# A convolution and a two-layer dense net on one core: dense part in two eras of seven weight blocks, array fills in unbroken chains

## The chip, the cores and the metric

One core of one Trainium2 chip runs the kernel. The metric is the device time of one execution in microseconds (us). TensorE is called PE here, VectorE DVE, ScalarE ACT, GpSimd POOL and SyncE SP, as the profile does. All large transfers are issued from SP's queue.

## The reference

Two branches share the input q of 2048 rows by 512 channels, and a gate per row mixes them:

```python
g = sigmoid((q * gate_w).sum(-1, keepdims=True))
k_shift = sum(k_pad[t:t + S] * shift_k[:, 3 - t] for t in range(4))   # short causal convolution
kv = k_shift * v
y = irfft(rfft(pad(kv)) * rfft(pad(ssm_k)))[:S] + kv * ssm_D          # long causal convolution, per channel
a = q * y
b = relu(q @ w1) @ w2                                                 # w1 512 x 1792, w2 1792 x 512
out = g * a + (1 - g) * b
```

Everything is float32.

## The kernel before, in words

**Dense part.** q is taken as four chunks of 512 rows, w1 and w2 as 14 blocks of 128 (f). For exactness each float32 operand is split into a high part (a cast to fp32r, on ACT, L247) and a low rest (a subtraction on DVE, L250), and each product is three matmuls: high by high, high by low, low by high. `mlp1(c, f)` (L308) multiplies chunk c by block f of w1: 12 matmuls of 512 columns into one bank. `mlp1_out` (L322) takes it out: relu on ACT as hh (L326), the rest on DVE as hl (L329). `mlp2(c, f)` (L335) multiplies hh and hl by block f of w2 for four row tiles s, three matmuls each (L341 to L343), and adds onto four banks m20 to m23 that stay open over all 14 f of a chunk. All 28 split weight blocks stay in SBUF. When a chunk is done, ACT copies its four banks out (L349) and SP stores them to a scratch tensor bd; they are loaded again near the end. The last chunk stays in its banks.

**Convolution.** It is a Fourier transform of length 2 x 2048 in steps. Stage 1 (`conv_h`, `conv_x`, `stage1`, L380 to L389): for eight pieces c, the filter (h) and the product k_shift * v (x, made on DVE in L432 to L448) are multiplied by a constant; two fills of the array each, four banks, which ACT copies to SBUF as ev and SP stores to scratch sa. Middle (`conv_mid`, eight groups g): two fills f_h, two fills f_x (L476), the complex product on DVE (L506 and L513), and the inverse iv, two fills (L524), copied out as bv by DVE and ACT and stored to scratch sb. End (`conv_end`): one fill per row tile (y, L586), two tiles at a time; then DVE gates (L595) and finishes (`finish`, L548), and SP stores the row tile to out. The stages are kept apart by their scratch: the middle begins when all of sa is stored, the end when all of sb is.

A **fill** here is a set of matmuls in which the array is cut into smaller arrays (64 x 128, 64 x 32, 32 x 64 or 128 x 64) that work together on 512 columns in full float32; a dense matmul uses it as one 128 x 128. There are 32 fills in stage 1, 48 in the middle, 16 at the end.

**What sets the order.** Everything is entered into a `Plan` (L79 to L188) with an engine, an assumed duration, a rank, its dependencies, and what it takes and gives of each buffer kind (`room`). `order()` plays this through: whenever an engine is free, the ready operation of lowest rank whose buffers are there is issued. The sequence that results is built as it stands; on the chip each engine works through its sequence in order and waits only for data and buffers. Convolution fills rank before dense matmuls (rank 0 and 1), so the dense part fills the time in between. PSUM's eight banks are four of kind cv (fills, mlp1 and warm-up) and m20 to m23.

The first two w1 blocks (G = 2) are loaded cut by k as wf, so that `mlp1_first` (L291) can start on the first quarter of the data; 13 matmuls on zeros (L610) run ahead of it.

Of the kernel before, what the change touches and what calls it, by code (L numbers as in the profile page):

```python
# [78 lines left out]
class Plan:  # L79

# [5 lines left out]
    def add(self, eng, dur, rank, fn, deps=(), take=(), give=(), dma=0, fifo=(), tiles=False):  # L86
        rank = tuple(_flat(rank))
        op = dict(tiles=tiles, eng=eng, dur=dur, rank=rank, fn=fn, take=tuple(take), give=tuple(give), dma=dma, fifo=tuple(fifo),
                  wait=0, next=[], n=len(self.ops))
# [8 lines left out]

    def order(self):
# [4 lines left out]
        out, soon, mode = [], [], False  # L104
# [9 lines left out]
        while True:  # L114
            for eng, ops in ready.items():
# [3 lines left out]
                held = ()  # L119
                if eng == "PE" and any(o["rank"][0] == 1 and not o["take"] for o in ops):  # L120
                    held = {t for o in ops + soon if o["rank"][0] == 0 and len(o["take"]) > 1 for t in o["take"]}
                for op in ops:
                    if best is not None and op["rank"] >= best["rank"]:
                        continue
                    if any(self.room[t] <= op["take"].count(t) - 1 for t in op["take"]):
                        continue
                    if any(self.turn[q][0] != op["n"] for q in op["fifo"]):
                        continue
                    if op["rank"][0] and any(t in held for t in op["take"]):
# [7 lines left out]
                ops.remove(op)  # L137
                for t in op["take"]:
# [6 lines left out]
                if eng == "PE":  # L145
                    if op["tiles"] and not mode:
# [15 lines left out]
            while events and events[0][0] <= now + 1e-9:  # L162
                _, _, what, op = heapq.heappop(events)
                if what == "go":
                    if op in soon:
                        soon.remove(op)
# [5 lines left out]
                for o in op["next"]:  # L172
# [4 lines left out]
                    if not o["wait"]:  # L177
                        s = 0 if near else SAFE.get(o["eng"] + str(int(o["rank"][0] != 0)) if o["eng"] == "PE" else o["eng"], 0)
                        if o["eng"] == "PE" and not near and now < PE_START and o["rank"][0] == 0:
                            s += 1.5  # L180
                        if s:
                            if o["eng"] == "PE":
                                soon.append(o)
# [16 lines left out]
TILES = 0.88  # L200
SWITCH = 0.33
# [3 lines left out]
def build(tc, wf, xp, qn, kn, vn, hn, dn, sh, gw, w1, w2, cs1, ccc, cib, out):  # L205
    nc = tc.nc
    queue = dict(SP=nc.sync, ACT=nc.scalar)
# [11 lines left out]
    bd = dram.tile([16, P, D], F32, name="bd")  # L219

    room = {"raw": RAW, "x": XB, "cv": 4, "hh": HHB, "m20": 1, "m21": 1, "m22": 1, "m23": 1, "o": OB, "in": IN, 
            "cc": 2, "acc": ACC, "tmp": TMP, "ev": EV, "r": RB, "ha": HAB, "p": PB, "bv": BVB,
            "br": BRB, "t": TB, "b": BB, "q": 4}
# [10 lines left out]
    def bank(key, tag="cv"):  # L234
        T[key] = pm.tile([P, D], F32, tag=tag, bufs=room[tag], name="_".join(map(str, key)))
        return T[key]

    rows = lambda x: x.rearrange("p (r d) -> p r d", d=D)
# [3 lines left out]
    def loaded(key, src, rank, p=None, tag="raw"):  # L242
        return add("SP", ISSUE["SP"], rank, lambda: nc.sync.dma_start(tile_of(key, tag, p=p), src), take=[tag], dma=ROW, fifo=[tag])

    def parted(key, rank, after, hi, lo, take=(), give=()):
        def h():
            nc.scalar.copy(hi(), T[key])  # L247

        def l():
            nc.vector.tensor_tensor(lo(), T[key], T[key[0], "h", *key[1:]].bitcast(F32), op=OP.subtract)  # L250

        a = add("ACT", act_time(D), rank, h, [after], take)
        if key[:2] == ("x", 0):
            xhigh[key[1:]] = a
        return add("DVE", dve_time(D), rank, l, [a], (), give)

    xdone, wdone, xhigh = {}, {}, {}

    def load_x(c, k, rank):
        key = ("x", c, k)  # L260
        ld = loaded(key, xp[c, k], rank - 3, mp)
        xdone[c, k] = parted(key, (0, rank), ld, lambda: tile_of(("x", "h", c, k), "xh", dt=F32R, bufs=XB, p=mp),
                             lambda: tile_of(("x", "l", c, k), "xl", dt=F32R, bufs=XB, p=mp), ["x"], ["raw"])

    def load_w(i, f, rank):
        key = ("w", i, f)
        ld = loaded(key, (w1, w2)[i][f], rank - 3, mp)
        wdone[i, f] = parted(key, (1, rank), ld, lambda: tile_of(("w", "h", i, f), f"w{i}h{f}", dt=F32R, bufs=1, p=wp),
                             lambda: tile_of(("w", "l", i, f), f"w{i}l{f}", dt=F32R, bufs=1, p=wp), (), ["raw"])

    def load_first(k, rank):
        key = ("g", k)
        ld = add("SP", ISSUE["SP"], rank, lambda: nc.sync.dma_start(tile_of(key, "ev")[:, :G * P], wf[k]), take=["ev"], dma=ROW * G // 4)

        def h():
            (nc.vector.tensor_copy if k == 0 else nc.scalar.copy)(tile_of(("g", "h", k), f"gh{k}", w=G * P, dt=F32R, p=wp), T[key][:, :G * P])

        def l():
            nc.vector.tensor_tensor(tile_of(("g", "l", k), f"gl{k}", w=G * P, dt=F32R, p=wp), T[key][:, :G * P],
                                    T["g", "h", k].bitcast(F32), op=OP.subtract)  # L280

        a = add("DVE", dve_time(G * P), -2000, h, [ld]) if k == 0 else add("ACT", act_time(G * P), -2000, h, [ld])
        wdone["g", k] = add("DVE", dve_time(G * P), -2000, l, [a], (), ["ev"])
        wdone["gh", k] = a

    def part(h, f, k):
        if f < G:
            return T["g", h, k][:, f * P:(f + 1) * P]
        return T["w", h, 0, f][:, k * P:(k + 1) * P]

# [446 lines left out]
```

## Time and profile before

| what | value |
|---|---|
| runs of the kernel | 426.11, 427.23, 427.33 us; median 427.23 |
| span of the profiled execution, first to last instruction | 424.4 us (its time with what lies around the span isn't listed) |
| PE busy, matmul instructions | 416.2 us, 98%; 2317 |
| DVE, ACT busy | 256.4 us, 60%; 120.3 us, 28% |
| transfers | 94.09 MB, mean 222 GB/s |
| mean granted TensorE clock | 0.999 |

Matmuls are pipelined, so their busy times overlap: the 1344 dense ones are listed with about 0.39 us each, while one starts every 0.227 us. What a matmul takes is therefore read from the distance between two starts in the timeline, not from its duration. In a row of the timeline the numbers are the start and the length of a group of like instructions; "x8" is their count, some records may be missing, and the brackets at the end give idle time before it and what ended it. In a row of the groups by line, the numbers behind the bar are busy us, mean ns of one, and idle time before with its releaser. In a row of the windows there stand the window, its length, then busy us and count for PE, weight loads, DVE, ACT and POOL, the clock, the share of the DMA engines and GB/s.

### The profile page before, as it was taken

To read this page: it belongs to the slowest core of one execution; us is meant where nothing else is said; L and a number is where in the kernel's file an instruction comes from. 1 tells how busy PE (TensorE), PEld (TensorE's weight loads), DVE (VectorE), ACT (ScalarE), POOL (GpSimd) and SP (SyncE) were. 2 spreads that over 40 slices of the span, in tenths; PEclk is the share of its full clock that TensorE was granted. 3 is DMA by queue.
4 is the path that set the end of the run, shared out by engine and by line. 5 is a ranking of instruction groups with operands and counts; after the bars stand their busy time and mean duration, and the time that the engine had idled before them with its cause. 6 is when DMAs were issued, how large, how long until landed. Compare 5 with 4: busy or idle time off the path is not lost.

```text
span 424.4 us, 6184 instructions
## 1 busy us (share of the span) xinstructions
PE 416.2 (98%) x2317; PEld 277.5 (65%) x2317; DVE 256.4 (60%) x394; ACT 120.3 (28%) x227; POOL 1.4 (0%) x6
## 2 busy tenths in 40 slices
PE   8999999999999999999999999999999999999994
PEld 7676767767767768555565655556577676776583
DVE  4599999979746101658584656748572356456412
ACT  4536454426433331121431112121132410111010
POOL 0000000000000000000000000000000000000000
PEclk9999999999999999999999999999999999999999
DMA  8998896978965448446886544645207898888002
GB/s 267 332 349 299 299 332 228 352 254 271 321 217 191 163 180 265 163 148 221 276 274 194 191 153 166 228 151 174 99 2 230 284 322 284 291 288 278 36 0 99
DMA packets 47503, 94.09 MB, mean 222 GB/s; under 512 B 5073, under 2 KB 5841, under 8 KB 47346
## 3 DMA queue, kind: packets, MB, share of 16 engines
q1 hardware_dynamic: 47410, 93.61, 65.0%
q8 instruction: 18, 0.29, 0.3%
q0 software_dynamic: 64, 0.10, 0.1%
q14 instruction: 11, 0.09, 0.1%
HBM read 61.18 MB, written 32.51 MB: 221 GB/s over the span
## 4 chain that ended last, share of the span: by engine, by line
PE 96%; DMA 2%; DVE 1%; issue 1%; ACT 0%; DVEq 0%; ACTq 0%
PE m L341 13%; PE m L314 12%; PE m L343 12%; PE m L315 12%; PE m L316 12%; PE m L342 12%; PE f_h L476 4%; PE iv L524 4%; PE f_x L476 4%; PE y L586 4%; PE s1h L380 3%; PE s1x L380 3%; PE m L298 2%; DMA sa<-ev 1%; PE warm L610 1%
## 5 line engine op out<-in xcount | busy, mean ns | idle before, releaser
L341 PE MATMUL m<-w1h_h,hh 128*128 128x512 f32 x224 | 92.0, 411 | 0.9 <-ACT hh L326 0.9
L343 PE MATMUL m<-w1h_h,hl 128*128 128x512 f32 x224 | 87.6, 391 | 0.1
L329 DVE SCALAR_TENSOR_TENSOR hl<-m,hh 128x512 fp32r<-128x512 f32 x56 | 38.5, 689 | 81.4 <-ACT hh L326 81.2
L342 PE MATMUL m<-w1l_l,hh 128*128 128x512 f32 x224 | 87.5, 391 | 0.0
L314 PE MATMUL m<-xh_h,w0h_h 128*128 128x512 f32 x192 | 76.6, 399 | 0.2 <-ACT ev L386 0.2
L326 ACT ACTIVATE hh<-m 128x512 fp32r<-128x512 f32 x56 | 33.4, 598 | 151.8 <-PE m L316 151.3
L315 PE MATMUL m<-xl_l,w0h_h 128*128 128x512 f32 x192 | 75.0, 390 | 0.0
L316 PE MATMUL m<-xh_h,w0l_l 128*128 128x512 f32 x192 | 74.8, 390 | 0.0
L341 PEld LDWEIGHTS m<-w1h_h,hh 128*128 128x128 f32 x224 | 42.0, 187 | 40.2 <-issue 28.9
L314 PEld LDWEIGHTS m<-xh_h,w0h_h 128*128 128x128 f32 x192 | 36.0, 188 | 19.9 <-issue 10.8
L343 PEld LDWEIGHTS m<-w1h_h,hl 128*128 128x128 f32 x224 | 42.1, 188 | 10.1 <-DVE hl L329 1.0
L342 PEld LDWEIGHTS m<-w1l_l,hh 128*128 128x128 f32 x224 | 42.1, 188 | 7.3
L316 PEld LDWEIGHTS m<-xh_h,w0l_l 128*128 128x128 f32 x192 | 36.1, 188 | 7.8
L315 PEld LDWEIGHTS m<-xl_l,w0h_h 128*128 128x128 f32 x192 | 36.1, 188 | 7.1
L438 DVE TENSOR_TENSOR acc<-acc,tmp 128x1024 f32<-128x1024 f32 x24 | 29.4, 1224 | 0.7
L506 DVE TENSOR_TENSOR p<-f_x,ha 128x512 f32<-128x512 f32 x32 | 19.9, 682 | 10.9 <-PE f_x L476 10.9
L535 DVE COPY bv<-iv 128x512 f32<-128x512 f32 x16 | 10.3, 686 | 21.8 <-PE iv L524 21.8
L386 ACT COPY ev<-s1x 128x512 f32<-128x512 f32 x32 | 16.8, 599 | 18.2 <-PE s1x L380 10.0
L386 ACT COPY ev<-s1h 128x512 f32<-128x512 f32 x32 | 16.8, 598 | 15.8 <-PE s1h L380 13.4
L435 DVE TENSOR_TENSOR tmp<-in,sht_sht 128x512 f32<-128x512 f32 x32 | 21.3, 682 | 0.0
L513 DVE TENSOR_TENSOR p<-p,ha 128x512 f32<-128x512 f32 x32 | 20.7, 681 | 0.0
L506 DVE TENSOR_TENSOR ha<-f_x,ha 128x512 f32<-128x512 f32 x32 | 19.8, 678 | 0.0
(59 smaller groups left out, 354.3 us busy)
## 6 DMA issues: line engine op xcount, KB each, us to landing
sa<-ev SPq DMA_DIRECT2D x64, 256.0 KB, 3.6
r_h<-sa SPq DMA_DIRECT2D x32, 256.0 KB, 3.8
r_x<-sa SPq DMA_DIRECT2D x32, 256.0 KB, 4.6
sb<-bv SPq DMA_DIRECT2D x32, 256.0 KB, 3.3
br<-sb SPq DMA_DIRECT2D x16, 512.0 KB, 5.3
raw<-w SPq DMA_DIRECT2D x26, 256.0 KB, 4.8
in<-kn SPq DMA_DIRECT2D x10, 512.0 KB, 6.0
raw<-xp SPq DMA_DIRECT2D x16, 256.0 KB, 3.9
```

Of the source, the lines that this page charges most:

```text
L314: mm(ps, part("h", f, k), T["x", "h", c, k], start=k == 0, stop=False)
L315: mm(ps, part("h", f, k), T["x", "l", c, k], start=False, stop=False)
L316: mm(ps, part("l", f, k), T["x", "h", c, k], start=False, stop=k == 3)
L326: nc.scalar.activation(tile_of(("hh", c, f), "hh", dt=F32R, p=mp, bufs=HHB), T["m1", c, f], AF.Relu)
L329: nc.vector.scalar_tensor_tensor(tile_of(("hl", c, f), "hl", dt=F32R, p=mp, bufs=HHB), T["m1", c, f], 0.0, T["hh", c, f].bitcast(F32), op0 ...
L341: mm(ps, T["hh", c, f][:, z], T["w", "h", 1, f], start=f == 0, stop=False)
L342: mm(ps, T["hh", c, f][:, z], T["w", "l", 1, f], start=False, stop=False)
L343: mm(ps, T["hl", c, f][:, z], T["w", "h", 1, f], start=False, stop=f == NF - 1)
L386: nc.scalar.copy(tile_of(("ev" + t, c, half, r), "ev"), T["s1" + t, c, half, r])
L438: nc.vector.tensor_tensor(T["acc", c], T["acc", c], T[dst], op=OP.add)
L476: mm(ps[b][32 * j:32 * j + 32, :], T[k("cc")][at, 64 * j + 32 * o:64 * j + 32 * o + 32], T[k("r", t, j // 2)][at, (j % 2) * D:(j % 2 + 1) ...
L506: tt(src if o else tile_of(k("p", i, b), "p"), T[k("f", "x", o, b)], src, op=OP.mult)
```

## The change

- **Eras.** The 14 blocks are taken as two eras of seven (`ERAS`). Era 0 goes through chunks 0 to 3, era 1 through 3 to 0. Within a chunk first `mlp1` for seven f, then `mlp2(era, c, s)` for each row tile s: its seven f, 21 matmuls, in one go. Era 0's row tile is copied to SBUF (y, ACT), era 1's is added to it (DVE); for the very last chunk the sum is made with the gate. bd and its transfers go. x is loaded and split a second time for chunks 2, 1 and 0. Split weights lie in rings of eight (WB), and era 1's take the places of era 0's.
- **Banks.** The dense part has two banks (m), fills have six (cv); only the first four w1 blocks (G = 4, was 2) use cv.
- **Chains.** `Plan.chain` ties fills together: once the first is issued, PE gets nothing else until the last. Stage 1: filter and x of a piece, four fills. Middle: iv of the group before, then f_h and f_x of this one, six fills. End: four row tiles, four fills.
- The planner's assumed numbers change with it, and its rule that held banks back for fills goes. Buffer counts: EV 7 (was 4), HAB 4 (was 8), TMP 1 (was 2), hh 7 (was 3), TB 6, BRB and QB 5.

```diff
+    def chain(self, ops):
+        ops[0]["rest"] = tuple(ops[1:])
+        for o in ops[1:]:
+            o["member"] = True
...
-                held = ()
-                if eng == "PE" and any(o["rank"][0] == 1 and not o["take"] for o in ops):
-                    held = {t for o in ops + soon if o["rank"][0] == 0 and len(o["take"]) > 1 for t in o["take"]}
                 for op in ops:
+                    if eng == "PE":
+                        if live and op is not live[0]:
+                            continue
+                        if not live and op["member"]:
+                            continue
...
-TILES = 0.88
-SWITCH = 0.33
+TILES = 0.865
+SWITCH = 0.19
...
-    room = {"raw": RAW, "x": XB, "cv": 4, "hh": HHB, "m20": 1, "m21": 1, "m22": 1, "m23": 1, "o": OB, "in": IN, 
+    room = {"raw": RAW, "x": 4, "cv": 6, "m": 2, "hh": HB, "o": OB, "in": IN, "cc": 2, "acc": ACC, "tmp": TMP, "ev": EV, "r": RB,
...
+    ERAS = [range(0, NF // 2), range(NF // 2, NF)]
+    CHUNKS = [list(range(NCHUNK)), list(range(NCHUNK))[::-1]]
...
-    def mlp2(c, f):
-        i = c * NF + f
-        for s in range(4):
-            def go(s=s):
+    def mlp2(era, c, s):
+        at[0] += 1
+        prev = None
+        fs = ERAS[era]
+        z = slice(s * P, (s + 1) * P)
+        for f in fs:
+            def go(f=f):
+                ps = bank(("m2", era, c, s), "m") if f == fs[0] else T["m2", era, c, s]
+                mm(ps, T["hh", era, c, f][:, z], T["w", "h", 1, f], start=f == fs[0], stop=False)
+                mm(ps, T["hh", era, c, f][:, z], T["w", "l", 1, f], start=False, stop=False)
+                mm(ps, T["hl", era, c, f][:, z], T["w", "h", 1, f], start=False, stop=f == fs[-1])
+
+            prev = add("PE", 3 * MM, (1, at[0], f), go, [hdone[era, c, f], wdone[1, f], prev], ["m"] if f == fs[0] else (),
+                       (["hh"] if s == 3 else []) + (["w2"] if s == 3 and c == CHUNKS[era][-1] else []))
+        n, i = 4 * c + s, at[0]
+        if era == 0:
+            def keep():
+                nc.scalar.copy(tile_of(("y", n), f"y{n}", p=mp), T["m2", era, c, s])
...
+        elif c != CHUNKS[1][-1]:
+            def plus():
+                nc.vector.tensor_tensor(T["y", n], T["m2", era, c, s], T["y", n], op=OP.add)
...
+    def stage1(c, rank, parts):
...
+                m = add("PE", TILES, (0, rank), go, deps if not ops else [ops[-1]], ["cv"] * 2, give if r == R - 1 else (), tiles=True)
+                ops.append(m)
...
+        plan.chain(ops)
...
+        ivp = lambda: link(2 * TILES, lambda: inverse(g - 1), deps, ["cv"] * 4, ["p"] * 4 + ["cc"])
...
+        if g and IV_FIRST:
+            put_iv(g - 1, ivp())
...
+            f = link(TILES, lambda o=o: rounds("h", o), deps, ["cv"] * 2 + ["ha"] * 2, ["r"] * 2 if o else ())
...
+            fx = link(TILES, lambda o=o: rounds("x", o), deps, ["cv"] * 2 + ([] if o else ["p"] * 4), ["r"] * 2 if o else ())
...
+            m = add("PE", TILES, (0, 700.0 + ns[0]), go, [chain[-1]] if chain else deps, ["cv"], ["br"], tiles=True)
+            chain.append(m)
...
+    for m in range(4):
+        conv_end(order_n[4 * m:4 * m + 4], p3)
...
-G = 2
+G = 4
```

What stands on PE around an inverse of the middle part, before: the inverse's last matmuls (iv), two dense groups of mlp2 (m), and then the first of f_x.

```order
L524 MATMUL iv_0_1705<-p_1_0_1625,cc_1484 64x512
L524 MATMUL iv_0_1706<-p_1_0_1625,cc_1484 64x512
L341 MATMUL m_1_2_1153<-w1h_h_10_708,hh_10_1559 128x512
L342 MATMUL m_1_2_1153<-w1l_l_10_719,hh_10_1559 128x512
L343 MATMUL m_1_2_1153<-w1h_h_10_708,hl_10_1571 128x512
L341 MATMUL m_1_3_1160<-w1h_h_10_708,hh_10_1559 128x512
L342 MATMUL m_1_3_1160<-w1l_l_10_719,hh_10_1559 128x512
L343 MATMUL m_1_3_1160<-w1h_h_10_708,hl_10_1571 128x512
L476 MATMUL f_x_0_1_1741<-r_x_1_1611,cc_1534 32x512
```

And in the changed kernel, at the inverse of group 1:

```order
L554 MATMUL iv_1_1893<-p_1_1_1813,cc_1484 64x512
L554 MATMUL iv_1_1894<-p_1_1_1813,cc_1484 64x512
L554 MATMUL iv_1_1895<-p_1_1_1813,cc_1484 64x512
L498 MATMUL f_h_0_2_1918<-r_h_2_1792,cc_1740 32x512
L498 MATMUL f_h_1_2_1919<-r_h_2_1792,cc_1740 32x512
L498 MATMUL f_h_0_2_1918<-r_h_2_1792,cc_1740 32x512
L498 MATMUL f_h_1_2_1919<-r_h_2_1792,cc_1740 32x512
L498 MATMUL f_h_0_2_1918<-r_h_2_1807,cc_1740 32x512
L498 MATMUL f_h_1_2_1919<-r_h_2_1807,cc_1740 32x512
```

The dense matmuls between have moved out: f_h of group 2 follows iv of group 1 at once, in a different cut of the array, and f_x of group 2 follows f_h.

On DVE the first steps of the kernel, before (gh and gl are the high part and the rest of the first w1 blocks, xl the rest of x):

```order
L276 CAST gh_h_108<-ev_78 128x256
L279 TENSOR_TENSOR gl_l_110<-ev_78,gh_h_108 128x256
L250 TENSOR_TENSOR xl_l_0_120<-raw_0_76,xh_h_0_102 128x512
L250 TENSOR_TENSOR xl_l_1_126<-raw_1_94,xh_h_1_114 128x512
L279 TENSOR_TENSOR gl_l_132<-ev_96,gh_h_122 128x256
L250 TENSOR_TENSOR xl_l_2_139<-raw_2_98,xh_h_2_129 128x512
```

And in the changed kernel, where w0h_h_g and w0l_l_g are the first w1 blocks' parts:

```order
L260 TENSOR_TENSOR xl_l_0_0_103<-raw_0_0_75,xh_h_0_0_99 128x512
L257 CAST w0h_h_g_107<-ev_g_77 128x512
L260 TENSOR_TENSOR w0l_l_g_111<-ev_g_77,w0h_h_g_107 128x512
L260 TENSOR_TENSOR xl_l_0_1_121<-raw_0_1_93,xh_h_0_1_109 128x512
L260 TENSOR_TENSOR w0l_l_g_131<-ev_g_95,w0h_h_g_117 128x512
L260 TENSOR_TENSOR xl_l_0_2_141<-raw_0_2_97,xh_h_0_2_127 128x512
```

The subtraction of x now stands ahead of the first cast of weights, and that cast is twice as wide.

At the end DVE has, before, the last hl and the four row tiles of the last chunk:

```order
L329 SCALAR_TENSOR_TENSOR hl_12_3632<-m_3_12_3610,hh_12_3627 128x512
L329 SCALAR_TENSOR_TENSOR hl_13_3661<-m_3_13_3640,hh_13_3656 128x512
L548 SCALAR_TENSOR_TENSOR o_3687<-m_3_0_3076,gs_3528,t_3529 128x512
L548 SCALAR_TENSOR_TENSOR o_3692<-m_3_1_3086,gs_3537,t_3538 128x512
L548 SCALAR_TENSOR_TENSOR o_3699<-m_3_2_3095,gs_3568,t_3569 128x512
L548 SCALAR_TENSOR_TENSOR o_3702<-m_3_3_3101,gs_3573,t_3574 128x256 x2
```

And in the changed kernel:

```order
L326 SCALAR_TENSOR_TENSOR hl_0_13_3673<-m_1_0_13_3647,hh_0_13_3668 128x512
L580 SCALAR_TENSOR_TENSOR o_3694<-m_1_0_0_3664,gs_3481,t_3482 128x512
L580 SCALAR_TENSOR_TENSOR o_3719<-m_1_0_1_3690,gs_3538,t_3539 128x512
L580 SCALAR_TENSOR_TENSOR o_3744<-m_1_0_2_3715,gs_3566,t_3567 128x512
L580 SCALAR_TENSOR_TENSOR o_3765<-m_1_0_3_3740,gs_3575,t_3576 128x256 x2
```

The instructions are the same kind, but each of the four now reads a bank that is finished 21 matmuls after the one before it, where it was three.

More of the change, by code (lines that the diff above doesn't have):

```diff
@@ L103, in order @@
         pipe = 0.0
-        out, soon, mode = [], [], False
+        out, mode, live = [], False, []
         for op in self.ops:
@@ L137, in order @@
                 ops.remove(op)
+                if live and op is live[0]:
+                    live.pop(0)
+                if op["rest"]:
+                    live = list(op["rest"])
                 for t in op["take"]:
@@ L145, in order @@
                 if eng == "PE":
-                    if op["tiles"] and not mode:
+                    if op["tiles"] != mode:
                         free += SWITCH
@@ L246, in h @@
         def h():
-            nc.scalar.copy(hi(), T[key])
+            (nc.scalar.copy if first == "ACT" else nc.vector.tensor_copy)(tile_of(hi, tag + "h", dt=F32R, bufs=bufs, p=p), T[key])
         def l():
[L250 to L255, printed above, removed]
@@ L495, in conv_mid @@
+        if g and not IV_FIRST:
+            put_iv(g - 1, ivp())
         d = dve_time(D)
```

416 lines of the change are left out of this document (205 added, 211 removed).

## The prediction

> **What bounds the kernel now.** First the page: is one engine busy throughout, and does the chain that ended last run along it?
>
> ```profile
> span 424.4 us, 6184 instructions
> PE   8999999999999999999999999999999999999994
> PEclk9999999999999999999999999999999999999999
> PE 96%; DMA 2%; DVE 1%; issue 1%; ACT 0%; DVEq 0%; ACTq 0%
> ```
>
> TensorE (PE) is busy in every slice but the first and the last, at a full granted clock, and 96% of the chain lies on it. So the time is the sum of what PE is given, plus a start and a tail. What PE is given, and what each kind costs, comes from the timeline: a start-to-start distance is what one matmul really takes (its printed length overlaps the next). First plain dense work, and a pair of fills L586 in it:
>
> ```profile
> 343.75 0.39 PE L314 MATMUL m<-xh_h,w0h_h 128*128 128x512 f32 x1
> ...
> 346.47 0.39 PE L341 MATMUL m<-w1h_h,hh 128*128 128x512 f32 x1
> ...
> 346.92 0.39 PE L343 MATMUL m<-w1h_h,hl 128*128 128x512 f32 x1
> 347.24 1.94 PE L586 MATMUL y<-br,ibt_ibt 128*64 128x512 f32 x8
> 349.11 0.50 PE L341 MATMUL m<-w1h_h,hh 128*128 128x512 f32 x1
> ```
>
> From 343.75 to 346.47 twelve matmuls start: 0.2267 us each. Now the other fills: one alone, then two together, in a stretch without waits:
>
> ```profile
> 172.28 0.40 PE L343 MATMUL m<-w1h_h,hl 128*128 128x512 f32 x1
> 172.60 1.09 PE L476 MATMUL f_h<-r_h,cc 64*32 64x512 f32 x16
> 173.62 0.50 PE L341 MATMUL m<-w1h_h,hh 128*128 128x512 f32 x1
> 173.96 0.39 PE L342 MATMUL m<-w1l_l,hh 128*128 128x512 f32 x1
> 174.19 0.40 PE L343 MATMUL m<-w1h_h,hl 128*128 128x512 f32 x1
> 174.52 1.95 PE L476 MATMUL f_x<-r_x,cc 64*32 64x512 f32 x32
> 176.40 0.50 PE L341 MATMUL m<-w1h_h,hh 128*128 128x512 f32 x1
> 176.74 0.40 PE L342 MATMUL m<-w1l_l,hh 128*128 128x512 f32 x1
> ...
> 186.98 0.39 PE L343 MATMUL m<-w1h_h,hl 128*128 128x512 f32 x1
> 187.30 1.97 PE L524 MATMUL iv<-p,cc 32*64 32x512 f32 x32
> 189.20 0.50 PE L341 MATMUL m<-w1h_h,hh 128*128 128x512 f32 x1
> ```
>
> ```profile
> 149.08 0.39 PE L343 MATMUL m<-w1h_h,hl 128*128 128x512 f32 x1
> 149.40 1.99 PE L380 MATMUL s1h<-in,s1c_s1t 64*128 64x512 f32 x8
> 151.32 0.50 PE L341 MATMUL m<-w1h_h,hh 128*128 128x512 f32 x1
> ```
>
> One fill: from 172.28 to 173.96 is 1.68 us, less two dense steps (0.45) 1.23 us. Two fills: from 174.19 to 176.74 is 2.55, less 0.45, 2.10. The second fill costs 0.87, so entering and leaving the array costs 1.23 - 0.87 = 0.36 us. It shows at both ends: the fill starts 0.32 to 0.33 after the last dense matmul, and the second dense matmul 0.34 after the first, where 0.227 is usual. The pairs of other shapes agree (last dense start to next dense start): 2.21 for f_x, 2.22 for iv, 2.19 for y, 2.24 for s1h. The bill before is 1344 dense matmuls, 96 fills and 56 visits to the array.
>
> **The change part by part.**
>
> *Visits to the array.* In the built order PE's fills stand in 56 unbroken groups before (16 of s1, 16 single f_h, 8 f_x, 8 iv, 8 y) and 21 after (8 of four fills, one of four, 7 of six, the last iv, 4 of four). The numbers of dense matmuls and fills stay. 35 visits fewer at 0.36: **-12.5 us**, all on PE and so on the path.
>
> *A change of shape inside a chain.* Seven chains go from iv (32 rows by 64 columns) straight to f_h (64 by 32). No row shows such neighbours. Two fills of one shape cost nothing extra (the f_x pair), dense to array and back costs 0.36: so 0 to 2.5 us for seven. One boundary, where a visit has two, is nearest to half a visit: 7 x 0.18 = **+1.2 us**. The Trainium skill, "TensorEngine Tiling (Array Packing)", Tiling Modes, Key Properties, says that a change of tiling mode, not of tile alone, drains the engine. By that rule the seven could cost a visit each and the sum be 1.3 us higher; the rows of f_h and f_x agree with it for dense to array, and for array to array no row here can tell.
>
> *Waits for banks inside a chain.* A middle chain fills twelve banks out of six. What empties them:
>
> ```profile
> 189.33 1.29 DVE L535 COPY bv<-iv 128x512 f32<-128x512 f32 x2 [4.10 <-PE iv L524]
> ```
>
> ```profile
> 189.37 1.07 ACT L533 COPY bv<-iv 128x512 f32<-128x512 f32 x2 [4.21 <-PE iv L524]
> ```
>
> ```profile
> 21.38 2.05 ACT L386 COPY ev<-s1h 128x512 f32<-128x512 f32 x4
> ```
>
> ```profile
> 170.07:320.00 149.93, 149.93 (x1194) 88.82 (x1194) 96.40 (x154) 34.77 (x62) 0.34 (x1) 1.00 0.52 173
> ```
>
> The iv fills end at 187.30 + 1.97 = 189.27. Two banks are out about 0.75 us later (VectorE's first copy, two copies in 1.29), all four after 1.35. The chain's second f_h fill wants the first two after one fill, 0.87, the first f_x fill the others after 1.74: 0.1 and 0.4 us to spare. VectorE takes its work in order and is 64% busy here (96.4 of 149.9 us); an operation of 0.69 just begun can cost up to 0.6 per chain. I take 0.64 x 0.23 = 0.15 for each of eight, **+1.2 us**, between 0 and 4.6. A first-stage chain fills eight banks; ScalarE empties four in 2.05 us, so the first two are out 1.1 us after their fill, and the fourth fill wants them after 1.74: 0.6 to spare, at nothing if at most one other operation of 0.6 lies ahead on ScalarE.
>
> *Two banks for the dense part.*
>
> ```profile
> L329 DVE SCALAR_TENSOR_TENSOR hl<-m,hh 128x512 fp32r<-128x512 f32 x56 | 38.5, 689 | 81.4 <-ACT hh L326 81.2
> L326 ACT ACTIVATE hh<-m 128x512 fp32r<-128x512 f32 x56 | 33.4, 598 | 151.8 <-PE m L316 151.3
> L438 DVE TENSOR_TENSOR acc<-acc,tmp 128x1024 f32<-128x1024 f32 x24 | 29.4, 1224 | 0.7
> ```
>
> A w1 block holds a bank for 12 matmuls, 2.72 us, and the bank must be empty again within the 2.72 of the next block: 0.60 on ScalarE and 0.69 on VectorE, 1.3 with little between. One operation of 1.22 ahead on VectorE still fits (2.5); a second doesn't. For the some twenty blocks beside the shift products I put **+0.8 us**, between 0 and 3. A row tile takes 21 matmuls, 4.8 us, and one copy: covered.
>
> *The start.*
>
> ```profile
> 3.40 0.62 ACT L247 CAST xh_h<-raw 128x512 fp32r<-128x512 f32 x1 [1.38 <-DMA raw<-xp]
> 3.71 0.29 DVE L276 CAST gh_h<-ev 128x256 fp32r<-128x256 f32 x1 [2.57 <-DMA ev<-wf]
> ...
> 4.15 1.19 PE L298 MATMUL m<-xh_h,gh_h 128*128 128x512 f32 x2
> ```
>
> ```profile
> 13.58 0.39 PE L341 MATMUL m<-w1h_h,hh 128*128 128x512 f32 x1
> ```
>
> At 13.58 27 dense matmuls have started, 6.1 us of work: 7.5 us are lost. Now VectorE's first step is the subtraction of x (it waits for the cast that ends at 4.02 and takes 0.7), and only then comes the cast of the first weights, twice as wide. The first matmul moves from 4.15 to about 5.3. But 48 instead of 24 then run on the first data, and three further w1 blocks before any second weight, so the wait for the first hh and hl before 13.58 is covered. With the clock slow until about 7 (two starts took about 1 us), the 48 end near 17.0, of which 10.9 is work: 6.1 lost. I take **-0.8 us**; +2 if the slow stretch lasts longer behind the gap, -1.5 if not.
>
> *The tail.*
>
> ```profile
> 417.46 4.25 SPq L552 DMA_DIRECT2D out<-o  x5
> ...
> 418.30 0.39 PE L343 MATMUL m<-w1h_h,hl 128*128 128x512 f32 x1
> ...
> 419.63 1.54 DVE L548 SCALAR_TENSOR_TENSOR o<-m,gs,t 128x512 f32<-128x512 f32 x3 [1.52 <-DMA out<-o]
> ```
>
> The last matmul ends at 418.69, the span at 424.4: 5.7 us. Four row tiles end there together, and VectorE waits 1.52 for one of two output buffers. After the change they end 4.8 us apart, so only the two halves of the last tile remain: 0.9, and the same 3.2 from VectorE's end (421.17) to the end. 4.1 instead of 5.7: **-1.5 us**.
>
> *Beside PE, at nothing.* Between the first ha and the last bv VectorE has 170 instructions for 154; at 96.4/154 = 0.63 each 106 us, in the 139 us that PE needs for 414 dense matmuls and the chains there: 77% busy, the cover holds. From the last iv to the first y, waits for stores and loads lie behind 96 dense matmuls (21.8 us):
>
> ```profile
> 317.04 1.90 PE iv L524 x32
> ```
>
> ```profile
> 324.28 0.63 SPq L564 DMA_DIRECT2D br<-sb  x1
> ```
>
> The first br load goes out 5.3 us after iv's end (318.94). The first chain of y now needs four tiles' br and most of their q, 2.75 MB; at the 284 GB/s of the page in that slice 9.7 us, with 2 to land 17.0 us: 4.8 to spare. The store and reload of twelve tiles (6.3 MB) go, twelve x loads (3.1 MB) come.
>
> *Sum.* -12.5 + 1.2 + 1.2 + 0.8 - 0.8 - 1.5 = -11.6 us. The span would be 424.4 - 11.6 = 412.8. The profiled execution's own time isn't shown; the runs' median, 427.2, lies 2.8 above the span, and I keep that: **415.6 us**.
>
> **The rivals.**
>
> *Emptying the banks sets the chains (17%).* The spare of 0.1 and 0.6 us fails where two operations lie ahead, which six fills in a row make likelier. At 0.6 in each of the 8 middle chains and the 8 first-stage ones that is 9.6 us, less the 1.2 counted: 424.0; at half of it, 419. For it speaks that ScalarE alone empties the first stage; against it, ScalarE's 35 of 150 us in the middle. The same page of the Trainium skill, Performance Considerations, PSUM Bottleneck, warns that tiling speeds TensorE up but not the emptying of its banks, so that this may become the limit; by that rule this case is the likely one, while in the trace f_x and iv, two fills on four banks, run without a gap.
>
> *The products come late, slower than before (4%).* From one middle chain to the next there are as few as 42 dense matmuls, 9.5 us, plus the 1.2 between the end of the first f_x fill and the dense work. Twelve dependent VectorE operations and three others lie in it: 15 x 0.63 = 9.4. At 0.81 us per operation, or four more operations ahead, all spare is gone; each chain then stops PE. Two us more for each of eight is 16 us: 431.6, slower. It decides against me from 1.5 us a chain. Against it: the wider gaps have 48 to 60 matmuls.
>
> *The start starves (6%).* All seven second weights must be there for the first row tile, not one per 5 us.
>
> ```profile
> GB/s 267 332 349 299 299 332 228 352 254 271 321 217 191 163 180 265 163 148 221 276 274 194 191 153 166 228 151 174 99 2 230 284 322 284 291 288 278 36 0 99
> ```
>
> The queue holds 7.3 MB up to the last of them; 267, 332 and 349 GB/s in slices of 10.6 us bring that by 24 us, casts make it 27; the order wants it at 17.0 + 60 x 0.227 = 30.6. Below 240 GB/s PE stops; 4 us lost give 419.6.
>
> *The change doesn't do what it says*: excluded for the groups, since the order shows 21.
>
> **How the numbers follow.** Forecast 73%, the rivals 17, 4 and 6. The bounds of the sum are -12.5 - 1.5 - 1.5 at the bottom, 411.7, and at the top -12.5 + 2.5 + 4.6 + 3 + 2 - 1.5, 425.3, which needs all at their worst; with the rivals' 419 to 420 the range is 411.0 to 422.0. Faster by over 0.3% (1.3 us, about what a measurement of this kernel can tell from no change) takes in all cases but the late products and the far end of the first rival: 0.93, same 0.03, slower 0.04.
>
> **What would show it.** Right: 21 groups in PE's timeline; four fills in about 3.85 us, six in 5.6 to 5.9; last matmul to end 4.1. Wrong: gaps inside a chain with VectorE or ScalarE copies as releaser, or six fills over 6.2; PE waiting before iv for the L540 products; the first row tile waiting for w2's casts; a start loss over 8 us.

## The result, and the profile after

The changed kernel takes 410.56 us (median of 4 runs, 409.76 to 412.09), the kernel before 426.67 us beside it (median of 4, 425.41 to 427.33): a ratio of 0.963, 95% interval 0.960 to 0.966, 16.1 us less. Faster was forecast, but 415.6 us within 411.0 to 422.0: the gain is larger than said, and the time lies 0.4 us below the range.

The page of the changed kernel first, the same rows as were shown of before:

```profile
span 408.7 us, 6184 instructions
PE   7999999999999999999999999999999999999996
PEclk9999999999999999999999999999999999999999
PE 94%; DMA 3%; DVE 2%; ACT 0%; issue 0%; DVEq 0%; ACTq 0%
```

TensorE (PE) still sets the time, now over 408.75 us instead of 424.37. So the 15.6 us have to be found in what PE does. Next the timeline of PE around one first-stage chain and one middle chain; the first number is the start, and distances between starts are what is read:

```profile
40.53 0.39 PE L342 MATMUL m<-w1h_h,hl 128*128 128x512 f32 x1
40.84 1.99 PE L386 MATMUL s1h<-in,s1c_s1t 64*128 64x512 f32 x8
42.67 1.88 PE L386 MATMUL s1x<-acc,s1c_s1t 64*128 64x512 f32 x8
44.48 0.50 PE L340 MATMUL m<-w1h_h,hh 128*128 128x512 f32 x1
44.82 0.40 PE L341 MATMUL m<-w1l_l,hh 128*128 128x512 f32 x1
```

```profile
180.30 0.39 PE L342 MATMUL m<-w1h_h,hl 128*128 128x512 f32 x1
180.62 1.97 PE L554 MATMUL iv<-p,cc 32*64 32x512 f32 x32
182.52 1.99 PE L498 MATMUL f_h<-r_h,cc 64*32 64x512 f32 x32
184.26 1.96 PE L498 MATMUL f_x<-r_x,cc 64*32 64x512 f32 x32
186.15 0.50 PE L340 MATMUL m<-w1h_h,hh 128*128 128x512 f32 x1
186.49 0.39 PE L341 MATMUL m<-w1l_l,hh 128*128 128x512 f32 x1
```

From the last dense start before a chain to the second after it, less two dense steps of 0.227, four fills take 4.29 - 0.45 = 3.84 us and six 6.19 - 0.45 = 5.74. Five of the seven long chains take 5.72 to 5.75, all eight of the first stage 3.85. Two of the long ones wait: 6.55 and 6.22. This is the longest wait, on PE and then on ScalarE (ACT):

```profile
197.26 1.97 PE L554 MATMUL iv<-p,cc 32*64 32x512 f32 x32
199.17 1.09 PE L498 MATMUL f_h<-r_h,cc 64*32 64x512 f32 x16
200.87 1.09 PE L498 MATMUL f_h<-r_h,cc 64*32 64x512 f32 x16 [0.62 <-ACT bv L565]
```

```profile
199.72 0.62 ACT L257 CAST w1h_h<-raw 128x512 fp32r<-128x512 f32 x1 [2.40 <-DMA raw<-w]
200.24 1.07 ACT L565 COPY bv<-iv 128x512 f32<-128x512 f32 x2
```

ScalarE sits idle for 2.40 us, up to 199.72, waiting for a late load of weights, while iv ends at about 199.2; the cast of that load stands ahead of the copy out of the bank in its order, and so the second f_h fill starts at 200.87 instead of 200.03. Not the copying is slow, the queue is.

The other wait, 0.48 us in the chain that starts at 286.74, stands behind VectorE (DVE). Four subtractions of x run ahead of its two copies out of iv's banks, which so start 2.39 us after iv instead of 2.06, and the rest of the second f_h fill follows the end of the second copy:

```profile
286.73 2.49 DVE L260 TENSOR_TENSOR xl_l<-raw,xh_h 128x512 fp32r<-128x512 f32 x4
289.13 1.28 DVE L567 COPY bv<-iv 128x512 f32<-128x512 f32 x2
```

```profile
290.46 0.63 PE L498 MATMUL f_h<-r_h,cc 64*32 64x512 f32 x7
```

The start and the end:

```profile
1.19 3.14 PE L648 MATMUL warm<-zero_zero 128*128 128x256 f32 x13 [1.19 <-DVE zero_zero L643]
5.28 1.17 PE L296 MATMUL m<-xh_h,w0h_h_g 128*128 128x512 f32 x4 [0.95 <-DVE w0h_h_g L257]
6.29 1.08 PE L296 MATMUL m<-xl_l,w0h_h_g 128*128 128x512 f32 x4
...
16.27 0.39 PE L310 MATMUL m<-xh_h,w0h_h 128*128 128x512 f32 x1
```

```profile
404.60 0.39 PE L342 MATMUL m<-w1h_h,hl 128*128 128x512 f32 x1
```

```profile
405.03 0.48 DVE o L580
405.51 0.39 DVEq L767
```

At 16.27 us 48 dense matmuls have started, 10.9 us of work: 5.4 us are lost, where 7.5 were. The last matmul ends at 405.0, and the span ends 3.8 us later, where it was 5.7: VectorE takes the last tile at once, in two halves.

Between these two ends PE's time can be added up from the timeline in both kernels. "Groups" is the sum over all visits to the array, from the last dense start before to the third after, less three dense steps.

| part | before | after | difference |
|---|---|---|---|
| lost at the start | 7.5 | 5.4 | -2.1 |
| groups of fills (56, 21) | 104.4 | 93.4 | -11.0 |
| what the dense matmuls between take beyond 0.2268 each | 1.9 | 1.3 | -0.6 |
| last matmul's end to the span's end | 5.7 | 3.8 | -1.9 |
| sum | | | -15.6 |

The second row holds the two waits of 1.3 us after, and before 0.4 us in two first-stage groups (those at 19.82 and 54.35 take 2.25 and 2.42 us, the other fourteen 2.13). The third row holds one wait of 0.6 us after (behind 370.16, for VectorE) and 0.2 before; the rest, 1.7 against 0.7, comes with the visits: the first dozen dense matmuls behind one are up to 9 ns slower each, about 0.03 us for each visit.

### The profile page after: what moved, and what is told of

Read it like the earlier page. It is cut to its first block, busy times and chain, and to the rows that moved or that the text cites. A ratio compares the mean times of both kernels' runs of the same rounds, so it can differ in the third digit from the quotient of the medians.

```text
span 408.7 us, 6184 instructions
## 1 busy us (share of the span) xinstructions
PE 401.8 (98%) x2317; PEld 283.5 (69%) x2317; DVE 274.2 (67%) x420; ACT 128.2 (31%) x241; POOL 1.4 (0%) x6
## 4 chain that ended last, share of the span: by engine, by line
PE 94%; DMA 3%; DVE 2%; ACT 0%; issue 0%; DVEq 0%; ACTq 0%
PE m L340 13%; PE m L341 12%; PE m L342 12%; PE m L310 11%; PE m L311 11%; PE m L312 11%; PE s1h L386 4%; PE f_h L498 4%; PE f_x L498 3%; PE s1x L386 3%; PE iv L554 3%; PE cy L619 3%; PE m L296 3%; DMA q<-qn 2%; DMA raw<-w 1%; DMA raw<-xp 1%
## 5 line engine op out<-in xcount | busy, mean ns | idle before, releaser
L340 PE MATMUL m<-w1h_h,hh 128*128 128x512 f32 x224 | 88.5, 395 | 0.0
L310 PE MATMUL m<-xh_h,w0h_h 128*128 128x512 f32 x160 | 63.4, 396 | 0.4 <-DVE gs L611 0.4
L311 PE MATMUL m<-xl_l,w0h_h 128*128 128x512 f32 x160 | 62.4, 390 | 0.0
L312 PE MATMUL m<-xh_h,w0l_l 128*128 128x512 f32 x160 | 62.3, 389 | 0.0
L310 PEld LDWEIGHTS m<-xh_h,w0h_h 128*128 128x128 f32 x160 | 30.0, 188 | 13.4 <-issue 5.7
L312 PEld LDWEIGHTS m<-xh_h,w0l_l 128*128 128x128 f32 x160 | 30.1, 188 | 6.4
L311 PEld LDWEIGHTS m<-xl_l,w0h_h 128*128 128x128 f32 x160 | 30.0, 188 | 5.9
L565 ACT COPY bv<-iv 128x512 f32<-128x512 f32 x16 | 8.6, 589 | 42.9 <-PE iv L554 36.0
L349 ACT COPY y<-m 128x512 f32<-128x512 f32 x16 | 9.4, 589 | 40.0 <-PE m L342 39.9
```

The costliest lines, as they stand in the source:

```text
L310: mm(ps, part("h", f, k), T["x", "h", xe, c, k], start=k == 0, stop=False)
L311: mm(ps, part("h", f, k), T["x", "l", xe, c, k], start=False, stop=False)
L312: mm(ps, part("l", f, k), T["x", "h", xe, c, k], start=False, stop=k == 3)
L340: mm(ps, T["hh", era, c, f][:, z], T["w", "h", 1, f], start=f == fs[0], stop=False)
```

## The experiments

The theory: PE is the bound, a visit to the array costs 0.36 to 0.38 us at its two ends and about 0.03 behind it, and the rest of the gain is the start and the tail. The main rivals: the new order of the dense part and its banks bring the gain, not the visits; or the banks, and not the visits, decide what a chain gives. Ratios are to the kernel before, run beside each.

**1. The visits, without their grouping.** Chains are cut, and the planner takes a dense operation after each fill where one is ready:

```diff
     def chain(self, ops):
-        ops[0]["rest"] = tuple(ops[1:])
...
+        return
...
-                    if best is not None and op["rank"] >= best["rank"]:
+                    key = (eng == "PE" and mode and op["tiles"], op["rank"])
+                    if best is not None and key >= (eng == "PE" and mode and best["tiles"], best["rank"]):
                         continue
```

> The changed kernel with its chains cut: after a fill the planner issues a dense operation first where one is ready, so 88 visits to the array instead of 21; eras, banks, transfers and fills stay. Theory (a visit costs 0.36 us at its two ends and about 0.03 in the dense matmuls behind it): 67 more visits at 0.39 are +26.1, the seven iv-to-f_h changes of shape (0.17 each) and the two waits for banks inside chains (1.3) go, so about +23.6 us: span near 432, slower than the kernel before. Rival (the gain comes from eras, row tiles and banks, not from visits): within 3 us of the changed kernel's 410.6.

Measured: 435.19 us, ratio 1.021 (1.020 to 1.023); 24.6 us above the changed kernel's 410.56, 23.6 was expected. A stretch of PE's timeline:

```profile
180.63 1.97 PE L553 MATMUL iv<-p,cc 32*64 32x512 f32 x32
182.53 0.50 PE L309 MATMUL m<-xh_h,w0h_h 128*128 128x512 f32 x1
182.87 0.39 PE L310 MATMUL m<-xl_l,w0h_h 128*128 128x512 f32 x1
183.10 0.40 PE L311 MATMUL m<-xh_h,w0l_l 128*128 128x512 f32 x1
183.43 1.09 PE L497 MATMUL f_h<-r_h,cc 64*32 64x512 f32 x16
184.45 0.50 PE L309 MATMUL m<-xh_h,w0h_h 128*128 128x512 f32 x1
184.78 0.39 PE L310 MATMUL m<-xl_l,w0h_h 128*128 128x512 f32 x1
```

Each visit shows its two ends again: 0.33 us from 183.10 to the fill, 0.33 between the first two dense matmuls behind it. No group waits for a bank and no dense gap is left, yet the 88 groups sum to 116.4 us against 93.4 in 21. Without the two waits and the seven changes of shape (1.3 us each, see experiment 6) that is 25.6 us for 67 visits, 0.38 each. A slow start (below) adds 2.2 us in this profile. With eras, row tiles and banks as in the changed kernel the time is above that of the kernel before: the visits are what the gain hangs on, and the first rival falls.

**2. The chain rule alone.** Only the first part of the edit above (chain returns at once).

> The changed kernel with the chain rule alone taken away; the fills still come ready together, so the built order has 28 visits instead of 21 (f_x apart from iv and f_h in seven groups). Theory: 7 x 0.39 = +2.7, less up to 1.3 if the waits inside chains go: +1.4 to +2.7 us, about 412 to 413.3. Rival (unbroken chains are what matters): clearly more, +5 or over. Rival (visits cost nothing): 0 or faster.

Measured: 413.09 us, ratio 0.970 (0.967 to 0.973), +2.5 us. The groups of a long chain: 3.13 for iv with one f_h fill and 2.96 for the other f_h fill with f_x's two, against 5.74 for all six in one; 94.5 us in 28 visits, with no wait for banks, against 93.4 with 1.3 of waits. So seven visits cost 2.4 here, and the 412 to 413.3 that were expected hold. In this profile there is also one dense wait of 1.6 (0.6 before) and a slower start (below), which make up the rest of its span of 413.1. That all fills of a group come ready together does most of the grouping; the rule that binds them brings the last seven visits.

**3. Fewer visits in the kernel before.** One constant: f_h's two fills as one operation.

```diff
-HS = 1
+HS = 2
```

> The kernel before with the two f_h fills issued as one operation (HS = 2): 52 visits instead of 56, four banks taken at once. Theory: 4 x 0.39 = -1.6 us, about 425.1, if no new wait for banks comes. Rival (with four fill banks a longer group waits for its banks and gives the gain back): 0 or slower, with gaps ahead of or within f_h.

Measured: 427.21 us, ratio 1.003 (1.002 to 1.004): no gain, a loss of 1.1. A miss of the theory alone, and a hit for the rival. PE behind two groups:

```profile
192.74 1.95 PE L476 MATMUL f_x<-r_x,cc 64*32 64x512 f32 x32
195.38 0.47 PE L314 MATMUL m<-xh_h,w0h_h 128*128 128x512 f32 x1 [0.69 <-DVE p L506]
...
208.55 1.97 PE L524 MATMUL iv<-p,cc 32*64 32x512 f32 x32
211.31 0.50 PE L314 MATMUL m<-xh_h,gh_h 128*128 128x512 f32 x1 [0.78 <-ACT bv L533]
```

f_h's pair does take 2.09 instead of 2 x 1.23 (in the new order four of the f_x pairs are split, so that 52 visits remain). But with four banks for fills and w1 blocks alike, the next w1 block stands in the queue for a bank that is being emptied: 0.7 to 0.9 each of three times, 2.3 us, more than the 1.5 that four visits give. Visits and banks belong together.

**4. The start alone, in the kernel before.**

```diff
-G = 2
+G = 4
```

> The kernel before with the first weights loaded for four blocks instead of two (G = 4), which is the changed kernel's start alone: 48 dense matmuls on the first data. Theory: the loss at the start falls from 7.5 to about 5.4 us, so -2.1 us, about 424.6, and the first matmuls run a start every 0.227 us. Rival (the slow first matmuls are the clock's and come with the run, not with G): the first starts lie 0.43 us apart until about 7 us as before, and the time moves by less than 1 us.

Measured: 428.91 us, ratio 1.006 (1.003 to 1.009): slower, where -2.1 was expected. The start itself did most of what was said: its first matmuls start every 0.227 us, and at 17.76 us 51 have started, 6.2 us lost instead of 7.5 (5.4 was expected). What takes it back stands later:

```profile
50.82 1.99 PE L380 MATMUL s1x<-acc,s1c_s1t 64*128 64x512 f32 x8
55.05 0.60 PE L314 MATMUL m<-xh_h,w0h_h 128*128 128x512 f32 x1 [2.24 <-ACT ev L386]
55.45 0.63 PE L315 MATMUL m<-xl_l,w0h_h 128*128 128x512 f32 x1
55.87 0.63 PE L316 MATMUL m<-xh_h,w0l_l 128*128 128x512 f32 x1
```

```profile
56.00:59.00 3.00, 3.00 (x9) 2.38 (x8) 2.67 (x4) 0.82 (x2) 0.00 (x0) 0.55 1.04 386
```

A w1 block waits 2.2 us for ScalarE to empty a first-stage bank, and behind this wait eight matmuls start 0.43 us apart, with the granted clock at 0.55 in that window; another wait, 1.3 us, stands behind 82.60. The stretch at the lower clock doesn't come in every execution: three of the six show a mean clock of 0.992 (428.95 to 430.50 us), three 0.999 (426.85 to 428.87). The plan as a whole had moved. So the start's part can't be had alone in that kernel.

**5. Four banks instead of six.**

```diff
-    room = {"raw": RAW, "x": 4, "cv": 6, "m": 2, "hh": HB, "o": OB, "in": IN, "cc": 2, "acc": ACC, "tmp": TMP, "ev": EV, "r": RB,
+    room = {"raw": RAW, "x": 4, "cv": 4, "m": 4, "hh": HB, "o": OB, "in": IN, "cc": 2, "acc": ACC, "tmp": TMP, "ev": EV, "r": RB,
```

> The changed kernel with four banks for fills and four for the dense part, as the split was before, chains unbroken. Theory (six banks are what lets a chain run through): after iv the first f_h fill must wait for the first two copies, 0.75 us less the change of shape, about 0.6 in each of 7 chains; in the first stage the third fill waits 0.28 and the fourth 0.1 in each of 8: together 7.3, less the one wait of the dense part (0.6): +6.7 us, about 417. Rival (the number of visits alone counts, banks are covered): within 1 us of 410.6.

Measured: 422.52 us, ratio 0.992 (0.989 to 0.995): 12.0 us of the 16.1 are gone again, where 6.7 were expected.

```profile
186.26 1.97 PE L554 MATMUL iv<-p,cc 32*64 32x512 f32 x32
188.99 2.01 PE L498 MATMUL f_h<-r_h,cc 64*32 64x512 f32 x32 [0.76 <-ACT bv L565]
190.93 2.01 PE L498 MATMUL f_x<-r_x,cc 64*32 64x512 f32 x32
192.87 0.50 PE L340 MATMUL m<-w1h_h,hh 128*128 128x512 f32 x1
```

f_h starts 2.73 us after iv instead of 1.90, and each pair after it takes 1.94 instead of 1.74 to 1.89: every long chain takes 6.82 instead of 5.74, the first one 4.73 instead of 3.81, each first-stage chain about 4.54 instead of 3.85. All groups: 106.1 us in the same 21 visits, against 93.4. The direction was right, the size twice what was worked out, since only the first wait of each chain had been counted in full and the later fills wait again. In the grouped kernel six banks are worth 12.7 us of groups, about as much as the 35 visits. Without them grouping still leaves this kernel 3.4 us ahead of the kernel before.

**6. One more change of shape per chain.** The changed kernel's own switch puts iv between f_h and f_x:

```diff
-IV_FIRST = True
+IV_FIRST = False
```

> The changed kernel with iv between f_h and f_x (its own switch IV_FIRST set False): two changes of shape in each of seven chains instead of one. Theory (a change of shape costs 0.17 us): six fills take 5.91 instead of 5.74 where nothing waits, 1.2 us in all; iv then needs four banks behind four that are being emptied, so 0.5 more in each chain can come: 411.8 to 415. Rival (iv to f_h costs nothing, the 0.17 is something else): 5.74 again.

Measured: 412.48 us, ratio 0.968 (0.965 to 0.970), groups of 5.92 to 5.96 (seven) instead of 5.74. The forecast holds. One change from 64 x 32 to 32 x 64 or back costs 0.19 us; a rival by which iv to f_h costs nothing falls. No chain waits for a bank in this order, so its groups sum to 93.4 us as before: what the two shape changes take, the two lost waits give. The span is longer by a slow start.

**7. Output buffers in the kernel before.**

```diff
-OB = 2
+OB = 3
```

> The kernel before with three output buffers instead of two (four don't fit beside the rest). Theory (at the end the row tile before the last waits for the store of the first): that wait, 1.52 us on VectorE, goes and the last tile waits a little for the first store instead: from the last matmul to the end 5.0 us instead of 5.7, so -0.7 us, 425.4. Rival (the tail is the last store alone): 5.7 as before.

Measured: 426.70 us, ratio 1.002 (1.001 to 1.004): no gain, where 425.4 was expected. The tail is shorter as said, 4.8 us from the last matmul's end (420.0) to the end (424.8) instead of 5.7:

```profile
417.99 2.11 DVE L548 SCALAR_TENSOR_TENSOR o<-m,gs,t 128x512 f32<-128x512 f32 x3 [4.74 <-PE m L343]
420.94 0.88 DVE L548 SCALAR_TENSOR_TENSOR o<-m,gs,t 128x256 f32<-128x256 f32 x2 [0.84 <-DMA out<-o]
```

The three first tiles go at once, the last still waits for a store. The 0.9 us are lost elsewhere in the new plan (two groups with a wait of 0.7 and 0.9). The end's cause is shown, its worth by itself is not.

**8. Warm-up up to the first product.** In the changed kernel PE idles 0.95 us between the warm-up and the first product.

```diff
-WARM = 13
+WARM = 17
```

> The changed kernel with 17 instead of 13 warm-up matmuls on zeros, so that TensorE is busy up to the first product at 5.3 us. Theory (the first product runs at a granted clock of half or of one by the run, since the gap of 1 us ahead of it may fall into the time over which activity is judged): without the gap the first 48 dense matmuls take 10.9 us in every run and the runs spread less: 409.5 to 410, spans all near 408.5. Rival (the clock's phase has nothing to do with the gap): the same spread, 408 to 411 in span.

Measured: 409.97 us (409.47 to 410.69), ratio 0.962 (0.960 to 0.965); spans of the five runs 407.7 to 408.9. Time and spans lie as forecast, and the spans spread over 1.2 us, where the changed kernel's spread over 2.3 in its first four runs and 2.1 in run 9; the times themselves are not clearly apart (0.960 to 0.965 against 0.961 to 0.967 in run 9).

**9 to 11. The changed kernel again, and two plans that expect loads later.** The first is the changed kernel as it is. Both others have 17 warm-up matmuls; one adds 1 us to each load that ScalarE or VectorE waits for, the other plans with 275 GB/s.

```diff
+                        if op["dma"] and o["eng"] in ("ACT", "DVE") and now > PE_START:
+                            s += 1.0
```

```diff
-DMA_RATE = 290000.0
+DMA_RATE = 275000.0
```

> The changed kernel once more, beside the next two on the same chip. Theory: the same 410.6 within its spread; some of its runs start with the 48 first matmuls at 0.45 us and end near 410.3 in span, others at 0.227 and near 408.5.

> The changed kernel with 17 warm-up matmuls, and with the planner assuming that ScalarE and VectorE get a load 1 us later than it did, so that casts of late loads no longer stand ahead of copies out of banks in the two engines' order. Theory (the two waits inside chains, 1.3 us, and the one of the dense part, 0.6, come from such casts and sums): these waits go, 1.9 us, and the time is 408 to 409. Rival (the order that results has other waits, since work moves later everywhere): 410 or over.

> The changed kernel with 17 warm-up matmuls, and with the planner assuming 275 instead of 290 GB/s for all transfers. Theory (late loads ahead of bank copies make the remaining waits): waits of 1.9 us go in part, 408.5 to 410. Rival: the plan is stretched where transfers are not late, and the time is 410 or over.

Measured: the changed kernel 411.57 us (0.964, 0.961 to 0.967), spans 408.3 to 410.4, as expected; late loads 412.34 us (0.967, 0.965 to 0.969), where 408 to 409 was expected; 275 GB/s 410.52 us (0.962, 0.960 to 0.964), where 408.5 to 410 was. The rivals of both have it right. In the last, all seven long chains run through in 5.72 to 5.75, so the waits behind late casts did go, but a first-stage chain waits 1.2 us in their place, behind four casts of x on ScalarE (71.05 to 73.22); with loads 1 us late a first-stage chain waits the same 1.2, one long chain still takes 6.22, and a dense wait of 1.3 for hl stands beside it. The waits that are left, some 2 us, move about with the plan. Of these versions none is clearly faster than the changed kernel.

On the start, the first rows of two profiles, of run 9 and of run 8:

```profile
5.46 2.05 PE L296 MATMUL m<-xh_h,w0h_h_g 128*128 128x512 f32 x4 [1.13 <-DVE w0h_h_g L257]
7.30 1.91 PE L296 MATMUL m<-xl_l,w0h_h_g 128*128 128x512 f32 x4
9.01 1.75 PE L296 MATMUL m<-xh_h,w0l_l_g 128*128 128x512 f32 x4
10.60 1.08 PE L296 MATMUL m<-xh_h,w0h_h_g 128*128 128x512 f32 x4
```

```profile
5.35 1.17 PE L296 MATMUL m<-xh_h,w0h_h_g 128*128 128x512 f32 x4 [0.62 <-DVE w0h_h_g L257]
6.35 1.08 PE L296 MATMUL m<-xl_l,w0h_h_g 128*128 128x512 f32 x4
```

The same instructions start 0.43 us apart until about 10.4 us in run 9 (four in 1.71 us, from 7.30 to 9.01), and 0.23 apart from the second in run 8. With 13 warm-up matmuls and G = 4, four of seven profiles begin slowly (runs 1, 2, 6 and 9) and three don't (the changed kernel's first, runs 4 and 5); with 17, one of three is slow, and for 1.3 us only (run 10). A slow start costs 2.5 us: in run 9 the 49th dense matmul starts at 18.79 instead of 16.27.

What the slow start is can be read from the list of granted clocks in each trace. It begins with an entry of full speed; the page counts what lies ahead of that entry as full too, which is why its row shows nothing. The first entry lies at 10.45 us in run 9, at 4.03 in run 8 and at 4.97 in the changed kernel's first profile, and in all 13 profiles undisturbed dense starts are 0.43 us apart ahead of it, where there are any, and 0.23 behind it. So the slow start is the clock. All entries but the last, which the end of the trace cuts short, last whole multiples of 3.413 us (in run 4 51.20, 3.41 and 365.23, in run 9 399.36). In every profile PE is idle for at most 0.65 us in the 3.413 us ahead of the first entry, and for 0.72 or more in the 3.413 us ahead of those; in the four slow profiles that earlier stretch holds the whole gap between warm-up and first product, 0.9 to 1.1 us. So the gap delays full speed when it falls whole into one such stretch. With 17 warm-up matmuls it is 0.1 to 0.6 us, and the latest first entry is at 6.53. That is three profiles, and how the stretches fall can't be set.

## Why the prediction was right and wrong

The mechanism holds: PE sets the time, and most of the gain is visits that are gone. The sum came out 5.0 us too high, and the steps that failed are sizes: the start (1.3 us), the step from span to time (1.0), the dense matmuls behind a visit (put at nothing, 1.0), the price of a visit (0.8), and waits in the first stage before (put at nothing), the dense part's banks and the tail (0.4 each); the chains' waits and changes of shape were 0.2 too low. The prediction had the means to see it: its own bill of the kernel before, 1344 x 0.2267 + 96 x 0.87 + 56 x 0.36 with 7.5 at the start and 5.7 at the end, comes to 421.6 us, 2.8 below the span of 424.4, and it was never added up.

- **The bound and the visits: right, the price a little low.** 35 fewer at 0.36 was -12.5; at 0.38 it is -13.3, and experiment 1 gives the same price with the opposite sign. The 0.36 is that of the middle's fills; at the first stage two visits of 2.13 became one of 3.85, 0.41 each.
- **Waits in the first stage before: left out.** The 0.4 us in the groups at 19.82 and 54.35 went with the change.
- **The change of shape: right.** +1.2 was taken from half a visit; 0.19 x 7 = +1.3 by experiment 6. The Trainium skill, "TensorEngine Tiling (Array Packing)", Tiling Modes, Key Properties, says that a change of mode drains the engine; the 0.19 agrees that array to array is such a change, and it costs half of what leaving and coming back does.
- **Waits for banks in chains: right in sum, partly in cause.** +1.2 was forecast, 0.81 + 0.48 = 1.3 came, in two chains instead of a little in all. The smaller is behind VectorE, as the text had in mind, the larger behind a cast of a late load on ScalarE, which it had not. That the sum fits is luck in part. The cover of the rest was real: experiment 5 shows what four banks would have cost, 12.7 us of groups. The same page of the Trainium skill, Performance Considerations, PSUM Bottleneck, warns that emptying the banks may become the limit. With six banks the trace bears it out for 1.3 us only, with four for 12.7 more.
- **Two banks for the dense part: right, a little high.** +0.8 against a net +0.4, one wait of 0.6 where 0.2 was.
- **The start: mis-sized.** The working gives 6.1 us lost instead of 7.5, which is -1.4; the text took -0.8 without saying why. It had the first matmuls slow until 7 us; the changed kernel's profile shows them at full rate from 5.28 and -2.1. This isn't the change's alone: in run 9 the same kernel loses 18.79 - 10.9 = 7.9 us at the start and gains nothing there. The step took one profile's slow stretch for a property of the kernel. In the kernel before, the clock hardly matters there: in runs 3 and 7 full speed comes at 5.92 and 4.41 instead of 7.29, and 7.5 and 7.6 us are lost all the same.
- **The dense matmuls behind a visit: left out.** 35 x 0.03 = -1.0; the rows shown (176.40 to 176.74) ended just where it begins.
- **The tail: mis-sized.** -1.5 against -1.9 (the working's own 4.1 instead of 5.7 is -1.6): the wait and the four tiles went as said, and from VectorE's end to the span's end it took 2.8 instead of 3.2.
- **Span to time: wrong.** 2.8 us were carried from the span to the median. Where a run's span is listed, its time is 1.7 to 1.9 above it (410.51 and 408.7; 435.31 and 433.5), 2.0 to 2.1 in run 11 alone. So the profiled execution before, with 424.37, was most likely the run of 426.11, and 1.0 us of the forecast was the spread of the runs before, put behind the span by mistake.
- **The range: too narrow below.** Its lower end gave the start a bound of -1.5 and gave none to the visits, the tail and the step from span to time, as if these were known. The bottom of its sum, -15.5, is close to the -15.6 between the two spans; what puts the time below the range is the 1.0 us behind the span. The start, the visits, the tail, the matmuls behind a visit and the 1.0 us all err on one side.
- **The rivals.** Emptying the banks didn't set the chains: they wait 1.3 us in all, where that rival had 9.6. Late products did not come: no iv waits for VectorE's products in the changed kernel. Nor did the start starve: dense matmuls run on every 0.227 us from 16.27 to the first chain at 40.84.

## What to carry to other kernels

Where one engine is full, list what it is given by kind, and price what lies between kinds from starts that are not disturbed: here 0.38 us per visit, times 56; then add the list up, and look for what is missing from the span. Grouping pays in full only with the buffers that let a group run through: in the kernel before, four visits fewer gave nothing (experiment 3), and the grouped kernel on four banks keeps 3.4 us of its gain (experiment 5). Six banks without grouping, at the 56 visits of before, were not run. A plan that is rebuilt from one changed constant moves its waits by 1 to 4 us, so an edit worth less than that has to be read from its own stretch of the timeline and not from the total; and a range needs bounds on the terms that seem known, and on the start, which one profile doesn't show.

## What the runs showed of the hardware

- A change from 128 x 128 to smaller arrays and back costs 0.36 us (64 x 32) to 0.41 (64 x 128), 0.38 on average; between 64 x 32 and 32 x 64 it costs 0.19; within one cut nothing (one, two and four fills of the first stage take 1.27, 2.13 and 3.85 us, 0.86 for each further one).
- The first dozen dense matmuls behind such a visit are slower by up to 9 ns each, about 0.03 us together.
- In run 4 PE is idle for 2.24 us between 51.88 and 55.29, and the 3.41 us behind that, up to 58.71, are listed at half the clock, with matmuls 0.43 us apart. Stretches of this length with up to 1.3 us of idle time, once the clock was full, were not followed by a lower one in any profile. The Trainium skill, "TensorE: Matmul & The Clock Gate", Part 1, What's actually happening, says that the clock is judged over free-running windows of about 3.4 us, and that it falls to half after an idle one. The entries of 3.413 us and the change of the start from run to run agree with it, while in run 4 a pause of 2.24 us was enough.
